# Fused top-k attention and GELU MLP: MLP pieces held behind the transposes, and x divided one or two rounds of DVE later, in the early slots

## The chip, the core and the metric

The kernel runs on one core of one Trainium2 chip. The core has five engines, each with a queue of its own that it works through in program order: PE (TensorE, matrix products; PEld is its loading of stationary operands), DVE (VectorE), ACT (ScalarE), POOL (GpSimd) and SP (SyncE, which here only issues DMAs). They wait for each other through semaphores. The metric is the device time of one execution in microseconds (us), smaller being better.

## The reference

Two stages, all in float32:

```python
scores = q @ k.T / sqrt(64)                       # 8 batches, 8 heads, 576 x 576
kth    = the 32nd largest score of each row
attn   = softmax(where(scores >= kth, scores, -1e9))
x      = (attn @ v) -> (4608 tokens, 512)          # heads side by side
g      = gelu_exact(x @ w_in)                      # w_in 512 x 2048
out    = g @ w_out                                 # w_out 2048 x 512
```

## The kernel before

**Items and slots.** The attention is cut into items: 128 rows of one pair of heads (576 rows make four items and a tail of 64 rows). A slot is one turn of the main loop and works on several items at different stages. In slot n of the first batch (`early_slot`, n = 0 to 17) the engines issue, in this order:

1. POOL adds the parts of one weight unit (`weights_add`, L235): the weights arrive as float32 words, are cut into two parts that PE multiplies well (ACT at L211, L214 and, in early units, L220; DVE at L216 in later units) and put together. A unit is two blocks of 128 x 512 of w_in or w_out; `made` is the set of units whose addition has been issued. 16 units are added in slots 1 to 16.
2. `larger(n+1)` on DVE (L420), `scores(n+2)`: PE multiplies q and k (the last keys at L347, the others at L384) and ACT copies the result (L355, L392).
3. `attend(n-2)`: PE multiplies the transposed exponentials with v into the tile o (L643), ACT copies o to xT (L661). The rows are not yet divided by their sum: a matmul with the inverse sums spreads these over o's other half (`dividing`, L656), and DVE multiplies (`copy_x`, L662). One MLP piece stands between o and the spread.
4. `top_k(n)`: DVE's search, a Python generator. A round is two `max` (L464: the eight largest of each head's row) and two `match_replace` (L467: take them out). There are six rounds for a paired item, the last ones without a replace; then DVE makes the inverse sums of item n-1 (`last`, L498) and the k-th value (L481, L482). The generator yields behind the first round; there the caller issues `copy_x` (so L662 stands behind one round in DVE's queue), and sets `ready`, the number of tokens whose x is complete.
5. `softmax(n-1)` for two heads on ACT (L511, L512), one part of the next weight unit (L211), two MLP pieces.
6. `transposes(n-1)`: PE transposes the exponentials in three pieces, two of four blocks (L573, one for each head) and the tail (L547), each followed by one MLP piece; ACT copies them to pt (L599, L557). The pieces of `transpose_qk` (L295, ACT's copies at L300) stand around them.
7. the other MLP pieces of the slot, the rest of the search, the weights' other parts, GELUs that have become due (`run_gelus`, ACT at L746, with an ACT table load ahead and one behind), `threshold` (POOL, L491, L492), from item 16 on `normalise` (POOL, L523), `sum_up` (POOL, L427), and the loads of the next slots.

**MLP pieces.** The MLP is a list `pieces` in a fixed order. A first-product piece (`l1_piece`, L726) is four matmuls of 128 x 128 in the first row tiles; a second-product piece (`full_piece`, L818) is one of 128 x 512. `mlp(n)` issues the next n pieces, as long as the slot's room (`left`) lasts, the piece's tokens are `ready`, and all its weight units are in `made`. With room left over, step 7 issues the rest. MLP work starts in slot 5 (`FIRST`). In slots 2 to 4 PE multiplies dummy tiles to stay busy.

**Rows of tokens.** In the first batch four consecutive items (the four pairs of heads) give a row tile of 128 tokens; in slots 5, 9, 13 and 17 `copy_x` completes such a row and `ready` goes up.

**Buffers.** Two score-sized PSUM tiles (`pr`, `l1`) and three banks; with MLP work only two banks (`z`, `y2`) go in turn to t_ps, o, tp_qk and tp_t, so the bank of o is free for the next but one user only when L662 has read it.

The slots in the trace of before, by the start of L420 on DVE, in us: slot 5 at 60.17, 6 at 69.24, 7 at 80.50, 8 at 90.16, 9 at 104.11, 10 at 117.96, 11 at 130.33, 12 at 140.40, 13 at 152.77, 14 at 164.97, 15 at 174.95, 16 at 186.18, 17 at 197.97, and the first slot of the later loop at 208.98. ACT's and PE's part of a slot starts about then. Behind the early slots a second loop works on the same stages in another order; there attention and MLP pieces share PE to the end.

Of the kernel before, what the change touches and what calls it, by code (L numbers as in the profile page):

```python
# [14 lines left out]
def kernel(  # L15
# [30 lines left out]
    NP = H // 2  # L46
# [106 lines left out]
    EARLY = NP * NM  # L153
# [14 lines left out]
    unit_in = UNIT_IN.get  # L168
# [30 lines left out]
    def parts(u):  # L199

        t, dst = words[u], weights_of(u)[3].bitcast(i32)
        return t[:, :, 0::2], t.bitcast(mybir.dt.int16)[:, :, 2::4], t[:, :, 1::2], dst

    def weights_size(u, part=None):


        if u not in words:
            return
        w, first, below, d = parts(u)
        if part != 1:  # L210
            nc.scalar.activation(below, first, func=AF.Prelu, bias=high, scale=2.0**-40, alpha=2.0**40)  # L211
        if part == 0:
            return
        nc.scalar.activation(d, below, func=AF.Prelu, bias=low, scale=2.0**59, alpha=2.0**-40)  # L214
        if on_dve(u):
            nc.vector.tensor_scalar(  # L216
                w.bitcast(i32), w.bitcast(u32), 2.0**-13, None, op0=ALU.mult
            )
        else:
            nc.scalar.activation(w.bitcast(i32), w.bitcast(u32), func=AF.Copy, scale=2.0**-13)  # L220

    def on_dve(u):

        return SLOT_OF[u] in ON_DVE

    def waits(u):

        return False

    made = set()  # L230

    def weights_add(u):
        if u in words:
            w, _, _, d = parts(u)
            nc.gpsimd.tensor_tensor(d, d, w.bitcast(i32), op=ALU.add)  # L235
        made.add(u)
# [172 lines left out]
    def paired(i):  # L409

        return PAIRED <= i < N and i not in SINGLE
# [5 lines left out]
    def larger(i):  # L417

        if paired(i):
            nc.vector.tensor_tensor(lists_of[i][:, 0], *halves_of(i), op=ALU.max)  # L420
# [16 lines left out]
    def top_k(i, last):  # L437


        stat_of[i] = st = {  # L440
            "first": work.tile([P, 2, 8], f32, tag="first", name="first"),
            "kth": work.tile([P, 2], f32, tag="kth", name="kth"),
            "neg": work.tile([P, 2], f32, tag="neg", name="neg"),
            "bias": work.tile([P, 2], f32, tag="bias", name="bias"),
            "den": work.tile([P, 2], f32, tag="den", name="den"),
            "rden": work.tile([P, 2], f32, tag="rden", name="rden"),
        }
        half_k = TOPK // 2
        top = work.tile([P, 2, TOPK - 8], f32, tag="top", bufs=1, name="top")
        low = work.tile([P, 2, half_k], f32, tag="low", bufs=1, name="low")  # L450
        into = [st["first"]] + [top[:, :, 8 * r : 8 * r + 8] for r in range(TOPK // 8 - 1)]
        if paired(i):
            t = lists_of.pop(i)
            rounds = [(t[:, 0], t[:, 0], x) for x in into]
            rounds += [(t[:, 1], t[:, 1], low[:, :, 8 * r : 8 * r + 8]) for r in range(half_k // 8)]
            ends = (len(into) - 1, len(rounds) - 1)
        else:
            s = S_of[i].rearrange("p (e n) -> p e n", e=2)
            t = work.tile([P, 2, S], f32, tag="lists", name="rest")
            rounds = [(s if r == 0 else t, t, x) for r, x in enumerate(into)]  # L460
            ends = (len(rounds) - 1,)
        for r, (src, dst, x) in enumerate(rounds):
            for e in range(2):
                nc.vector.max(x[:, e], src[:, e])  # L464
            if r not in ends:
                for e in range(2):
                    nc.vector.match_replace(dst[:, e], x[:, e], src[:, e], LOWEST)  # L467
            if r == len(rounds) - 1:
                last()
            if r == 0:  # L470
                yield

        if not paired(i):
            st["kth"] = top[:, :, TOPK - 9]
            return
        upper = top[:, :, half_k - 8 :]
        backwards = bass.AP(
            tensor=low.tensor, offset=low.offset + half_k - 1,
            ap=[list(low.ap[0]), [half_k, 2], [-1, half_k]],
        )  # L480
        nc.vector.tensor_tensor(upper, upper, backwards, op=ALU.max)  # L481
        nc.vector.tensor_reduce(  # L482
            st["kth"].rearrange("p (e x) -> p e x", x=1), upper, mybir.AxisListType.X, ALU.min
        )
# [9 lines left out]
    def inverse(i):  # L494
        if i < 0 or i >= N:
            return
        st = stat_of[i]
        nc.vector.reciprocal(st["rden"], st["den"])  # L498
# [7 lines left out]
    def softmax(i, e):  # L506

        if i < 0 or i >= N:
            return
        st, s = stat_of[i], row(i, e)  # L510
        nc.scalar.activation(s, s, func=AF.Prelu, bias=st["neg"][:, e : e + 1], scale=1.0, alpha=STEEP)  # L511
        nc.scalar.activation(  # L512
            s, s, func=AF.Exp, bias=st["bias"][:, e : e + 1], scale=1.0,
            accum_out=st["den"][:, e : e + 1],
        )
# [94 lines left out]
    def copy_x():  # L610
        while copies:
            copies.pop()()
# [83 lines left out]
    for base in range(0, NT, RING):  # L696
        whole = [(0, 256), (256, 256)] if base else [(t * P, P) for t in range(NM)]
# [317 lines left out]
    def run_gelus():  # L1015
        while waiting:
            u = waiting.pop(0)
            if u in HELD:
                gelus(u - 2)
            gelus(u)  # L1020
            if eager[0]:
                run_small(9)

    def run_ends():
        while ends:
            ends.pop(0)()

    def run_small(room):

        while summing:  # L1030
            sums(summing.pop(0))
            room -= 4
        while small and room > 0:
            n, f = small.pop(0)
            f()
            room -= n
# [10 lines left out]
    pieces = [x for y in blocks for x in y]  # L1047
    done = [0]

    def mlp(n):  # L1050
        for _ in range(n):
            if done[0] >= len(pieces) or pieces[done[0]][0] > ready[0] or left[0] <= 0:
                return
            if not all(w in made for w in pieces[done[0]][1]):
                return
            pieces[done[0]][2]()
            done[0] += 1
            left[0] -= 1
            if eager[0]:
                run_gelus()  # L1060
                run_small(9)


    ready, left = [0], [0]
    SPREAD = (12, 30)

    def room_in(n):

        x = n - START - 1
        if n < SPREAD[0]:  # L1070
            return min(7 if n < 9 else 6, sum(sizes[:4]) - done[0])
        if n < SPREAD[1]:
            ends = sum(sizes[:4]), sum(sizes[: SPREAD[1] - START - 1])
            part = (n - SPREAD[0] + 1) / (SPREAD[1] - SPREAD[0])
            return min(10, round(ends[0] + part * (ends[1] - ends[0])) - done[0])
        if x >= len(sizes):
            return 0
        return sizes[x] + (1 if x % 2 == 0 else -1)
# [62 lines left out]
    def early_slot(n):  # L1141

        left[0] = room_in(n) if n >= FIRST else 0
        begun[0] = n >= FIRST
        if not waits(unit_in(n)):
            weights_add(unit_in(n))
        larger(n + 1)
        scores(n + 2)
        product = attend(n - 2)
        mlp(1)  # L1150
        while dividing:
            dividing.pop()()
        searches = top_k(n, lambda: inverse(n - 1))
        next(searches)
        copy_x()
        ready[0] = n_tok[0]
        softmax(n - 1, 0)
        softmax(n - 1, 1)
        u = unit_in(n + 1)
        if u is not None:  # L1160
            weights_size(u, 0)
        mlp(2)
        if n < FIRST:
            keep_busy(6 if product else 12, ident)
        prep = prep_in.pop(n, [])
        for piece in prep[:1]:
            piece(None)
        tr = transposes(n - 1) if n - 1 < EARLY else []
        for piece in tr:
            piece()  # L1170
            mlp(1)
        for piece in prep[1:]:
            piece(None)
            mlp(1)
        if n < FIRST:
            keep_busy(8, ident)
        smaller(n + 1)
        add_small(n - 1)
        mlp(left[0])
        run_ends()  # L1180
        for _ in searches:
            pass
        if u is not None:
            weights_size(u, 1)
        run_gelus()
        threshold(n)
        normalise(n - 1)
        sum_up(n + 2)
        run_small(6)
        next_loads(n)  # L1190
# [5 lines left out]
    for n in range(LAST_EARLY + 1, ahead):  # L1196
# [16 lines left out]
        tr = transposes(n - 2)  # L1213
# [78 lines left out]
```

## Time and profile before

| what | value |
|---|---|
| time, median of 3 runs | 1569.61 us (1567.76 to 1569.66) |
| the profiled execution's own time | 1569.94 us |
| its span, first to last instruction | 1567.5 us |
| mean granted PE clock | 0.992 |
| span from 0 to 212 us | first batch, weights and the first MLP pieces |

The profile's rows read as follows. In order of time: start in us, duration in us, engine, line, operation, output<-input, shape, xcount of merged instructions, and in brackets the idle time of the engine before it with what ended it. Each float32 matmul is two records (x8 are four matmuls). In the waits view: who waited for whom, us in total, times, the longest. In the windows view: a stretch of the span and the busy time of each engine in it, then the clock granted to PE (1.00 is full), the DMA share and GB/s. The page's PEclk row cuts the span into 40 slices of 39.2 us; each digit is the granted clock in tenths.

### The profile page before, as it was taken

What the parts mean: (1) busy time and instruction counts of PE and PEld (TensorE: products, weight loads), DVE (VectorE), ACT (ScalarE), POOL (GpSimd) and SP (SyncE); (2) the same over time, 40 slices, a digit from 0 to 9 for tenths busy, and PEclk for the clock granted to TensorE, in tenths of its full rate; (3) what the DMA queues carried; (4) which work ended last, traced back from release to release, by engine and by line L of the source; (5) the groups of instructions that cost most, each with busy time, mean ns of one, the idle gap of its engine ahead of it and who ended that gap; (6) DMA issues with size and microseconds to landing.
All of it is one profiled execution on the core that took longest, in us unless ns stands there. A gap on an engine that the chain in (4) does not pass through costs nothing.

```text
span 1567.5 us, 28535 instructions
## 1 busy us (share of the span) xinstructions
PE 1521.3 (97%) x9478; PEld 1184.5 (76%) x9478; DVE 1335.6 (85%) x4605; ACT 1157.4 (74%) x2030; POOL 1096.1 (70%) x1253
## 2 busy tenths in 40 slices
PE   8979999999999999999999999999999999999998
PEld 6756667657777778887777778787777777787887
DVE  7978889899989997998989997988998998888700
ACT  6978867677777778777777778777777778777720
POOL 4646556556687877777787877786778786876732
PEclk9979999999999999999999999999999999999999
DMA  6432310011101111011200111001210111000000
GB/s 178 143 98 97 85 45 8 8 30 35 35 15 24 32 35 31 1 30 38 39 22 16 30 31 38 8 17 36 39 24 18 27 30 31 15 1 14 8 14 13
DMA packets 184243, 56.37 MB, mean 36 GB/s; under 512 B 175008, under 2 KB 175584, under 8 KB 184096
## 3 DMA queue, kind: packets, MB, share of 16 engines
q1 hardware_dynamic: 180720, 52.23, 14.1%
q10 hardware_dynamic: 3152, 2.00, 0.4%
q8 instruction: 74, 1.21, 0.3%
q14 instruction: 73, 0.60, 0.1%
q0 software_dynamic: 224, 0.33, 0.1%
HBM read 45.08 MB, written 9.44 MB: 35 GB/s over the span
## 4 chain that ended last, share of the span: by engine, by line
PE 71%; DVE 7%; POOL 6%; ACT 2%; issue 1%; SPq 0%; DMA 0%; DVEq 0%; POOLq 0%
PE h_ps L726 26%; PE y_ps L879 14%; PE o L643 7%; PE tp L573 6%; PE s_ps L384 5%; PE seven L877 2%; PE y_ps L818 2%; DVE top L464 2%; POOL s L523 2%; DVE rest L467 1%; PE tp_t L347 1%; PE y_ps L841 1%; PE y_ps L844 1%; PE o L672 1%; DVE lists L467 1%
## 5 line engine op out<-in xcount | busy, mean ns | idle before, releaser
L726 PE MATMUL h_ps<-xT,w_in_sb 128*128 128x256 f32 (+1 forms) x2688 | 530.6, 348 | 0.4 <-DVE xT L662 0.3
L726 PEld LDWEIGHTS h_ps<-xT,w_in_sb 128*128 128x128 f32 x2688 | 434.6, 191 | 65.3 <-issue 24.6
L464 DVE MAX8 top<-lists 128x8 f32<-128x288 f32 x798 | 323.8, 447 | 0.0
L523 POOL TENSOR_TENSOR s<-s,rden 128x1152 f32<-128x1152 f32 x128 | 269.1, 2102 | 0.3 <-DVE rden L498 0.3
L512 ACT ACTIVATE s<-s,bias 128x576 f32<-128x576 f32 x288 | 223.4, 776 | 12.0
L467 DVE MATCH_REPLACE8 lists<-top,lists 128x288 f32<-128x288 f32 x532 | 231.6, 443 | 0.0
L511 ACT ACTIVATE s<-s,neg 128x576 f32<-128x576 f32 x288 | 225.7, 784 | 4.2 <-POOL neg L491 4.0
L464 DVE MAX8 low<-lists 128x8 f32<-128x288 f32 x532 | 214.8, 446 | 0.0
L589 ACT COPY pt<-tp 128x1024 f32<-128x1024 f32 x128 | 130.0, 1016 | 101.8 <-PE tp L573 101.8
L504 POOL TENSOR_SCALAR den<-den 128x2 f32<-128x2 f32 x144 | 31.4, 218 | 237.6 <-ACT s L512 233.0
L435 POOL TENSOR_TENSOR lists<-lists 128x576 int32<-128x576 int32 x133 | 187.6, 1410 | 4.4
L427 POOL TENSOR_TENSOR lists<-s 128x576 int32<-128x576 int32 x133 | 187.0, 1406 | 0.0
L491 POOL TENSOR_SCALAR neg<-kth 128x2 f32<-128x2 f32 x133 | 85.2, 641 | 140.2 <-DVE kth L482 131.3
L573 PE MATMUL tp<-ident,s 128*128 128x128 f32 x1152 | 153.7, 274 | 5.5 <-ACT s L512 5.4
L643 PEld LDWEIGHTS o<-pt,raw_v 128*64 128x64 f32 x1440 | 93.1, 137 | 87.0 <-issue 46.8
L643 PE MATMUL o<-pt,raw_v 128*64 128x256 f32 (+1 forms) x1440 | 154.8, 362 | 0.0
L573 PEld LDWEIGHTS tp<-ident,s 128*128 128x128 f32 x1152 | 135.4, 142 | 23.9 <-ACT s L512 8.1
L392 ACT ACTIVATE s<-s_ps 128x1024 f32<-128x1024 f32 x127 | 124.9, 1026 | 21.9 <-PE s_ps L384 21.1
L384 PE MATMUL s_ps<-kt,qm 64*128 64x512 f32 x512 | 131.9, 625 | 4.5 <-ACT pt L589 2.9
L879 PE MATMUL y_ps<-w_out_sb,sum 128*128 128x256 f32 x448 | 133.2, 379 | 0.0
L498 DVE RECIPROCAL rden<-den 128x2 f32<-128x2 f32 x144 | 23.1, 160 | 118.2 <-POOL den L504 117.3
L467 DVE MATCH_REPLACE8 lists<-low,lists 128x288 f32<-128x288 f32 x266 | 115.9, 443 | 0.0
(168 smaller groups left out, 2756.3 us busy)
## 6 DMA issues: line engine op xcount, KB each, us to landing
raw_v<-in_v_dram SPq DMA_DIRECT2D x64, 128.0 KB, 2.4
w_out_sb<-in_moe_w_in_dram SPq DMA_DIRECT2D x14, 511.8 KB, 4.9
out_dram<-late SPq DMA_DIRECT2D x26, 256.0 KB, 2.1
raw_q<-in_q_dram SPq DMA_DIRECT2D x96, 64.0 KB, 2.1
raw_k<-in_k_dram SPq DMA_DIRECT2D x96, 64.0 KB, 2.1
w_out_sb<-in_moe_w_out_dram SPq DMA_DIRECT2D x10, 511.8 KB, 4.3
w_sum<-in_moe_w_out_dram SPq DMA_DIRECT2D x4, 511.8 KB, 5.5
raw_q<-in_q_dram SPq DMA_DIRECT2D x96, 8.0 KB, 1.9
```

Of the source, the lines that this page charges most:

```text
L384: nc.tensor.matmul(s_ps[:, e], lhsT=q_t[rows, :], rhs=kt[rows, 0:SM], start=True, stop=True)
L427: nc.gpsimd.tensor_tensor(t[:, 1].bitcast(i32), a.bitcast(i32), b.bitcast(i32), op=ALU.add)
L435: nc.gpsimd.tensor_tensor(both, both, top, op=ALU.subtract)
L464: nc.vector.max(x[:, e], src[:, e])
L467: nc.vector.match_replace(dst[:, e], x[:, e], src[:, e], LOWEST)
L511: nc.scalar.activation(s, s, func=AF.Prelu, bias=st["neg"][:, e : e + 1], scale=1.0, alpha=STEEP)
L512: nc.scalar.activation(s, s, func=AF.Exp, bias=st["bias"][:, e : e + 1], scale=1.0, accum_out=st["den"][:, e : e + 1],)
L523: nc.gpsimd.tensor_tensor(s, s, wide, op=ALU.mult)
L573: nc.tensor.transpose(tp[:, j * P : (j + 1) * P], s[:, first + j * P : first + (j + 1) * P], ident)
L643: nc.tensor.matmul(o[e * D : (e + 1) * D, 0:n], lhsT=vt[:, j, e, :], rhs=pt[:, e * NM + j if j < NM else 2 * NM, x], start=(j == 0), stop= ...
L726: nc.tensor.matmul(h_tile(u)[:, i, :], lhsT=w_in_sb[:, ko, f * P : (f + 1) * P], rhs=xT[:, ko, c0 : c0 + n], start=(ko == 0), stop=(ko == ...
L879: nc.tensor.matmul(acc[names][:, k], lhsT=lhsT, rhs=rhs, start=(j == 0 and k == 0), stop=(j == FT // 2 - 1 and k == 1),)
```

## The change

Two edits in `early_slot`, with a helper of each:

- At the start of a slot `known` becomes a copy of `made` as it was before this slot's weight unit is added. `mlp` takes a piece only if its units are in `known`; from the last transpose of the slot on (`known[0] = None`) it goes by `made` again. So pieces that need the unit added in the same slot come behind the transposes; pieces that don't need it stay where they were.
- `top_k` yields behind every round, and `early_slot` asks for three rounds ahead of `copy_x`, or for two where the slot completes a row of tokens (`whole`). The rounds themselves, their operands and their number stay.

`waits`, which always gave False, is removed. The lines behind it move up by four; lines are named as in the kernel before.

```diff
@@ top_k
-            if r == 0:
-                yield
+            yield
@@ mlp
-            if not all(w in made for w in pieces[done[0]][1]):
+            if not all(w in (known[0] or made) for w in pieces[done[0]][1]):
...
-    ready, left = [0], [0]
+    ready, left, known = [0], [0], [None]
@@ early_slot
-        if not waits(unit_in(n)):
-            weights_add(unit_in(n))
+        known[0] = set(made)
+        weights_add(unit_in(n))
...
         searches = top_k(n, lambda: inverse(n - 1))
-        next(searches)
+        whole = n - 2 < EARLY and (n - 1) % NP == 0
+        for _ in range(2 if whole else 3):
+            next(searches)
         copy_x()
...
         tr = transposes(n - 1) if n - 1 < EARLY else []
-        for piece in tr:
+        for x, piece in enumerate(tr):
             piece()
+            if x == len(tr) - 1:
+                known[0] = None
             mlp(1)
+        known[0] = None
```

More of the change, by code (lines that the diff above doesn't have):

```diff
@@ L224, in on_dve @@
         return SLOT_OF[u] in ON_DVE
-    def waits(u):
-        return False
     made = set()
```

## The prediction

> **What bounds the kernel now.** I read the page first, then the waits in the first batch (60 to 212 us), then that stretch in order of time, engine by engine.
>
> ```profile
> span 1567.5 us, 28535 instructions
> ...
> PE 1521.3 (97%) x9478; PEld 1184.5 (76%) x9478; DVE 1335.6 (85%) x4605; ACT 1157.4 (74%) x2030; POOL 1096.1 (70%) x1253
> ...
> PEclk9979999999999999999999999999999999999999
> ```
>
> PE is the bound. All its work is issued in program order, so whatever PE loses to waiting or to a low clock is paid at the end. It loses 1567.5 - 1521.3 = 46 us, and the granted clock is low in one slice only, the third (78 to 118 us). The edits touch the 18 early slots alone (to 209 us); behind them PE's order is unchanged and PE is the engine that the others follow. So I work out how much earlier PE arrives there.
>
> ```profile
> DVE xT L662 <- PE o L656: 24.6, 11, 4.2
> ```
>
> This is the wait that the second edit aims at: DVE stands 24.6 us in 11 stalls before the division of x. But a DVE stall costs time only where PE, or something that PE waits for, follows from it:
>
> ```profile
> 120.00:130.00 10.00, 10.00 (x93) 8.72 (x91) 7.34 (x28) 8.55 (x14) 4.17 (x5) 1.00 0.18 40
> ```
>
> The columns are PE, PEld, DVE, ACT, POOL busy, then the granted clock. PE is busy all of 10 us at full clock while DVE is busy 7.34: there DVE waits for PE, and ending its stall gives nothing. What can be gained lies in slots 6 to 9 (69 to 118 us), where PE idles and its clock falls:
>
> ```profile
> 80.60:84.00 3.40, 0.97 (x12) 0.49 (x9) 3.40 (x12) 3.32 (x8) 3.33 (x4) 1.00 0.12 22
> 84.00:101.00 17.00, 13.26 (x68) 10.15 (x67) 12.76 (x46) 10.33 (x17) 9.33 (x9) 0.60 0.37 124
> 104.50:107.90 3.40, 1.90 (x24) 1.07 (x20) 1.94 (x7) 3.37 (x5) 3.40 (x3) 1.00 0.00 0
> ...
> 111.30:114.70 3.40, 3.40 (x18) 3.40 (x18) 3.40 (x14) 3.35 (x7) 0.22 (x1) 0.50 0.47 189
> 142.00:145.40 3.40, 1.71 (x7) 0.74 (x8) 0.79 (x4) 3.39 (x8) 3.40 (x3) 1.00 0.00 0
> 145.40:148.80 3.40, 3.40 (x6) 1.25 (x6) 3.40 (x14) 3.30 (x5) 0.88 (x1) 0.51 0.81 279
> ```
>
> The clock falls behind 3.4 us in which PE was busy 0.97 us (at 84.0) and 1.71 us (at 145.4), not behind 1.90 us; it is back after a stretch that PE fills.
>
> **The change, part by part.** In the built programs PE's order differs in three slots only: in 6 and 8 four MLP pieces (16 matmuls) go behind the transposes, in 16 two pieces do. On DVE one instruction per slot moves back by one round (slots 5, 9, 13, 17) or two. ACT, POOL and SP keep their order, so no DMA issue passes another.
>
> Slot 5 (a whole row of tokens is ready, so its pieces read x at once):
>
> ```profile
> 62.75 1.38 PE L726 MATMUL h_ps<-xT,w_in_sb 128*128 128x128 f32 x10 [0.34 <-DVE xT L662]
> 62.61 0.81 DVE L464 MAX8 top<-lists 128x8 f32<-128x288 f32 x2
> ...
> 64.19 0.81 DVE L464 MAX8 top<-lists 128x8 f32<-128x288 f32 x2
> ```
>
> A round is 64.19 - 62.61 = 1.58 us. x now comes one round later, and PE, which already waits for it, **loses 1.58 us**. Nothing hides it, and DVE gains nothing, since it did not stall there.
>
> Slot 6:
>
> ```profile
> 73.17 0.78 ACT L512 ACTIVATE s<-s,bias 128x576 f32<-128x576 f32 x1
> ...
> 74.74 0.78 ACT L512 ACTIVATE s<-s,bias 128x576 f32<-128x576 f32 x1
> 73.49 2.10 PE L726 MATMUL y_ps<-xT,w_in_sb 128*128 128x128 f32 x16
> 75.43 0.60 PE L573 MATMUL tp<-ident,s 128*128 128x128 f32 x4
> 75.86 1.06 PE L726 MATMUL y_ps<-xT,w_in_sb 128*128 128x128 f32 x8
> ...
> 78.20 0.39 PE L347 MATMUL t_ps<-kt,qm 128*128 128x128 f32 x2
> ...
> 79.57 1.31 PE L643 MATMUL o<-pt,raw_v 128*64 128x128 f32 x20
> 82.83 0.77 ACT L512 ACTIVATE s<-s,bias 128x576 f32<-128x576 f32 x1
> 83.75 0.92 PE L573 MATMUL tp<-ident,s 128*128 128x128 f32 x4 [1.19 <-ACT s L512]
> ```
>
> ACT follows PE there and is 1.58 late too. Without a piece ahead of them the transposes wait for the two exponentials: the second starts at 74.74 + 1.58 = 76.3, its transposes 0.92 later (83.75 behind 82.83), at 77.25. Four transposes take 0.43 (75.43 to 75.86), the short ninth 0.1, and the 16 matmuls what is left of the 4.71 us from 73.49 to 78.20, some 3.65. Scores then start at 77.25 + 0.5 + 3.65 = 81.4, not 78.20: **3.2 late**. ACT stood behind PE there:
>
> ```profile
> 81.82 0.25 ACT L661 COPY xT<-o 128x128 f32<-128x128 f32 x1
> 91.51 0.27 ACT L661 COPY xT<-o 128x128 f32<-128x128 f32 x1 [0.82 <-PE o L643]
> 94.09 0.77 ACT L512 ACTIVATE s<-s,bias 128x576 f32<-128x576 f32 x1
> ...
> 94.87 1.21 ACT L211 ACTIVATE w_out_sb<-w_out_sb,high 128x1024 f32<-128x1024 int16 x1
> ```
>
> o starts 1.37 behind the scores (79.57 - 78.20) and takes 1.3: it ends at 84.05, and the copy starts there, not at 81.82. ACT and PE go through slot 7 hand in hand, so I carry **2.2 late** on: the copy of 91.51 comes at 93.7. DVE gets ahead, which nobody needs yet.
>
> Slot 8, where the gain is:
>
> ```profile
> 94.73 1.22 PE L726 MATMUL y_ps<-xT,w_in_sb 128*128 128x128 f32 x4 [2.63 <-POOL w_in_sb L235]
> ...
> 96.50 3.79 PE L726 MATMUL y_ps<-xT,w_in_sb 128*128 128x128 f32 x16
> ...
> 100.93 0.67 PE L573 MATMUL tp<-ident,s 128*128 128x128 f32 x4
> 101.17 0.58 ACT L300 COPY kt<-tp_qk 128x512 f32<-128x512 f32 x1 [5.09 <-PE tp_qk L295]
> 102.97 1.01 ACT L599 COPY pt<-tp 128x1024 f32<-128x1024 f32 x1 [1.21 <-PE tp L573]
> ...
> 107.58 1.09 ACT L746 ACTIVATE g<-y_ps 128x512 f32<-128x512 f32 x2
> ...
> 109.59 0.33 ACT L661 COPY xT<-o 128x128 f32<-128x128 f32 x1
> 109.97 0.44 PE L656 MATMUL o<-ident,rden 128*64 128x128 f32 x4 [3.57 <-ACT xT L661]
> ```
>
> Now PE waits 2.63 for the weights of that slot, multiplies at half clock (16 records in 3.79 us, in slot 6 in 2.10), and only at 100.93 transposes scores whose exponentials had started at 94.09 at the latest; from 102.97 ACT runs without a break to 109.59. Afterwards the spread follows o, and the second transposes come at 94.09 + 2.2 + 0.92 = 97.2. ACT's L211 (94.87 + 2.2, 1.2 long) ends at 98.2, the copy of keys takes 0.5, and the pt copy starts at 98.7: **4.3 early**. The four pieces run behind the tail transpose, from 98.0, at half clock (0.45 a matmul) until the clock returns. PE is full from 97.2, so it returns between about 100.6 and 104, by where in the 3.4 us steps PE stands; the pieces end at 103.1, 103.7 in the middle, or 104.6. The GELU of y_ps is due at 107.58 - 4.3 = 103.3 and waits for at most 1.3; scores and o (1.37 + 1.3) follow the pieces, so the copy of 109.59 comes at 105.8, 106.4 or 107.3: 3.8, 3.2 or 2.3 early. PE's wait of 3.57 is nearly gone, since o ends just before. So no empty stretch precedes slot 9, and the half clock of 111.3 to 114.7 falls away: it cost up to 1.7, but the transposes of that slot follow ACT's exponentials, so between 0 and 1.7 comes back; I take 0.9. The second round of slot 9 costs nothing: DVE reaches the division before the copy and still waits. At slot 10 PE is **4.7, 4.1 or 3.2 early**; I take 4.1. From there PE is full and DVE ahead, and the loads of w_out stand in SP's queue behind loads that follow PE's transposes, so they come as much earlier.
>
> Slot 16 and the end:
>
> ```profile
> 193.48 0.66 PE L573 MATMUL tp<-ident,s 128*128 128x128 f32 x4 [0.32 <-ACT s L512]
> 193.97 1.02 PE L818 MATMUL y_ps<-w_out_sb,g 128*128 128x512 f32 x2
> 195.05 0.66 PE L573 MATMUL tp<-ident,s 128*128 128x128 f32 x4
> ...
> 212.08 0.41 PE L550 MATMUL tp_t<-ident,s 128*64 128x128 f32 x2 [0.53 <-POOL s L523]
> ```
>
> The piece between the transposes filled their wait for the second exponential. It goes behind, the 1.08 us from 193.97 to 195.05 stay empty, and PE **loses 0.9** (ACT is at work without a break there, so nothing hides it). At 212.08 PE waited 0.53 for a POOL product that hangs on DVE's k-th value; DVE needs one round less behind its last division, so **0.5** returns. Sum: 1.58 and the rest of slots 5 to 9 make -4.1, then + 0.9 - 0.5 = **-3.7** (-4.3 to -2.8). The profiled execution took 1569.94 us, 2.4 more than its span; that gives 1566.2, and from the median of 1569.61, 1565.9.
>
> The Trainium skill bears on the clock ("TensorE: Matmul & The Clock Gate", Part 1: The HAM clock gate): a free-running window of about 3.4 us, half clock after an idle window, full clock after a busy one. The trace agrees with the window (3.4 us at half from 111.3, 17.0 = 5 x 3.4 from 84.0), but its clock fell without an idle one.
>
> **The rivals.** A: *the clock stays full*, if only a wholly empty step lowers it: no wait left in slots 7 and 8 is longer than 1.3 us.
>
> ```profile
> 87.53 2.08 PE L384 MATMUL s_ps<-kt,qm 64*128 64x512 f32 x4 [0.46 <-ACT pt L599]
> ```
>
> From these scores to the copy of 91.51 it is 3.98 at half clock, and would be some 2.4 (1.1 and 1.3): 1.6 less. The pieces end before the GELU is due, so the pt copy and all behind it come 5.9 early, and slot 10, with up to 1.1 of slot 9's clock, 7.0: -6.6, 1563.0. The page's rule gives this; the 0.97 and 1.71 above speak against it.
>
> B, the other side: *the clock falls already in slot 6.* Its emptiest 3.4 us (73.8 to 77.2) will hold some 1.6 us of PE work: 0.8 of a piece's four matmuls, 0.4 of spread (109.97), 0.4 of transposes. Below 1.71 the clock has fallen, at 1.90 not. If it falls there and returns only in slot 9: 16 matmuls at half (+3.6), scores and o of slot 7 (+1.7), all of slot 8's pieces at half (+1.4), slot 9 no better than now (+0.9): -3.7 + 7.6 = +3.9, 1573.5. Against it: the clock returns once PE fills 3.4 us, which these 16 matmuls do.
>
> C: *the delays of slots 5 and 6 eat the gain*: the late end (-2.8) and one 3.4 us step of half clock in slot 6 (+1.7): -1.1, 1568.5.
>
> D: *all DVE stalls are given back*: 1569.6 - 24.6 = 1545; against it stands the full PE of 120 to 130 us. That an edit does nothing is excluded: both move instructions in the built program.
>
> **How the numbers follow.** Forecast 0.56, A 0.08, B 0.10, C 0.24, D 0.02. About 0.2% (3.1 us) is what a measurement of this kernel can tell. Faster by more: forecast without its late end (0.52), A and D: 0.62. Within: C and that end, 0.28. Slower: B, 0.10. The range leaves out B and D: from A, 1563.0, to 1569.0, just above C.
>
> **What would show it.** PE's wait for x in slot 5 near 1.9 us; scores of slot 7 at 81.4; the pt copy of slot 8 near 98.7; no wait for POOL weights in slot 8; no half clock in slot 9; L662's stalls moved to slots 9, 12, 13, 17, not gone. Wrong would be: half clock before 84 (B), none at all (A), or a PE in slots 10 to 15 that isn't full.

## The result, and the profile after

The changed kernel takes 1561.15 us (median of 4 runs, 1559.38 to 1562.20); the kernel before took 1568.89 (4 runs, 1567.76 to 1569.66) beside it. The ratio is 0.995, interval 0.9933 to 0.9967: 5.2 to 10.5 us less. The forecast had the sign, and about half of the size: 3.7 less, range to 1563.0. A second comparison, on another chip, gave 0.9965 (0.9952 to 0.9979), 3.3 to 7.5 us less. The profiled executions of two runs below, `known8` and `after_again`, took 3162 and 2614 us; they and their traces are left out of every number that follows.

The page of the changed kernel, to be held against the first rows of the prediction:

```profile
span 1559.1 us, 28536 instructions
...
PE 1514.1 (97%) x9478; PEld 1178.0 (76%) x9478; DVE 1336.6 (86%) x4605; ACT 1157.0 (74%) x2030; POOL 1095.8 (70%) x1253
...
PEclk9999999999999999999999999999999999999999
```

PE is busy 7.2 us less (1521.3 - 1514.1) for the same instructions. So most of the gain shows up as work done at a higher clock; the third slice has lost its 7. What raised the clock is a question for the experiments. The lines of the changed kernel stand 4 or 5 lower: L657 is the division that was L662, L721 the MLP piece that was L726.

Where along the early slots does the time come from? PE's scores (t_ps) and ACT's pt copy serve as landmarks. The table gives the start of each in us, the forecast as the prediction worked it out (the time before plus its shift), and one experiment, `early_one`, which is told below.

| landmark | before | forecast | after | early_one |
|---|---|---|---|---|
| scores, slot 6 | 69.42 | 71.0 | 68.64 | 71.93 |
| scores, slot 7 | 78.20 | 81.4 | 79.06 | 82.35 |
| pt copy, slot 8 | 102.97 | 98.7 | 96.14 | 99.64 |
| scores, slot 10 | 118.65 | 114.6 | 110.89 | 114.37 |
| scores, slot 13 | 153.31 | | 146.44 | 148.66 |
| scores, slot 17 | 197.91 | | 191.87 | 194.07 |

The changed kernel left the forecast already in slot 5, and by slot 10 it was 3.7 us ahead of it. DVE's timeline has the reason, in a slot that the prediction never looked at. Before, slot 2, and the first instruction of slot 5:

```profile
35.23 0.29 DVE L662 TENSOR_TENSOR xT<-xT,o 128x128 f32<-128x128 f32 x1 [2.31 <-PE o L656]
...
60.17 0.75 DVE L420 TENSOR_TENSOR lists<-s 128x576 f32<-128x576 f32 x1
```

After, the same two and the division of slot 5:

```profile
35.77 0.28 DVE L657 TENSOR_TENSOR xT<-xT,o 128x128 f32<-128x128 f32 x1
...
57.54 0.75 DVE L416 TENSOR_TENSOR lists<-s 128x576 f32<-128x576 f32 x1
...
61.49 0.29 DVE L657 TENSOR_TENSOR xT<-xT,o 128x128 f32<-128x128 f32 x1
```

In slot 2 DVE had stood 2.31 us for o. With two rounds more ahead of the division that stall is gone, DVE enters slot 5 2.63 us earlier (60.17 - 57.54), and there the second round (1.58) is more than paid for: x is divided at 61.49, before it was at 62.42. PE's wait for x, which was to grow from 0.34 to 1.9, vanishes instead.

Slot 8 on PE after the change:

```profile
93.12 0.66 PE L568 MATMUL tp<-ident,s 128*128 128x128 f32 x4 [0.60 <-ACT s L507]
94.68 0.66 PE L568 MATMUL tp<-ident,s 128*128 128x128 f32 x4 [0.91 <-ACT s L507]
95.18 0.27 PE L542 MATMUL tp_t<-ident,s 128*128 128x128 f32 x1
95.29 3.74 PE L721 MATMUL y_ps<-xT,w_in_sb 128*128 128x128 f32 x32
98.86 0.39 PE L343 MATMUL t_ps<-kt,qm 128*128 128x128 f32 x2
```

The transposes follow the exponentials, the 32 records of the pieces come behind them without a wait for POOL, and at full clock (0.117 us each, where the forecast had them at half). The clock itself, in its own steps of 3.41 us (busy PE second, the granted clock third from the end). Before:

```profile
84.00:87.41 3.41, 2.43 (x11) 1.73 (x9) 3.41 (x13) 3.32 (x6) 2.80 (x3) 0.50 0.32 77
87.41:90.82 3.41, 3.29 (x16) 1.79 (x18) 3.38 (x12) 2.54 (x5) 1.09 (x2) 0.50 0.59 235
90.82:94.23 3.41, 1.28 (x16) 0.91 (x12) 1.67 (x7) 2.61 (x6) 3.41 (x3) 1.00 0.00 0
94.23:97.64 3.41, 2.91 (x13) 2.36 (x14) 0.95 (x4) 1.85 (x3) 2.03 (x3) 0.50 0.58 166
97.64:101.05 3.41, 3.41 (x18) 3.41 (x18) 3.41 (x14) 0.00 (x0) 0.00 (x0) 0.50 0.35 142
```

After:

```profile
83.59:87.00 3.41, 1.65 (x11) 1.22 (x11) 3.38 (x14) 3.38 (x7) 0.71 (x2) 0.99 0.59 228
87.00:90.41 3.41, 3.08 (x14) 1.57 (x16) 3.41 (x14) 2.69 (x5) 3.41 (x4) 0.51 0.00 0
90.41:93.82 3.41, 2.40 (x26) 1.51 (x22) 3.41 (x14) 2.60 (x7) 2.43 (x2) 1.00 0.33 100
```

The prediction read 84 to 101 us as one stretch at half clock. It was two stretches of two steps, with a full one between (90.82 to 94.23), and the second fell out of PE's wait for POOL in slot 8. After the change there is a single step at half in this stretch.

Behind slot 10 three things move the sum. In slot 16 the gap between the transposes appears as forecast (t_ps loses 0.83 from slot 16 to slot 17). The wait of 0.53 at 212.08 is gone, as forecast. And slot 12 brings one that was not seen. ACT's timeline after:

```profile
129.40 1.21 ACT L211 ACTIVATE w_out_sb<-w_out_sb,high 128x1024 f32<-128x1024 int16 x1 [2.25 <-DMA w_out_sb<-in_moe_w_out_dram]
130.51 0.57 ACT L296 COPY kt<-tp_qk 128x512 f32<-128x512 f32 x1
130.97 1.02 ACT L594 COPY pt<-tp 128x1024 f32<-128x1024 f32 x1
```

and PE's, behind ACT's copy of keys:

```profile
131.13 0.49 PE L343 MATMUL t_ps<-kt,qm 128*128 128x128 f32 x2 [1.74 <-ACT kt L296]
```

Before, ACT's wait for that load was 1.30, and PE's 0.81. PE arrives 7.76 us earlier at slot 10, but by slot 13 its lead is 6.87: 0.89 goes here.

The spans differ by 8.4 us (1567.5 and 1559.1), of which 6.8 are there at the pt copy at 207.53 (214.29 before). The last 1.6 is luck of the clock. In both kernels PE waits 2.4 us near the end; the clock falls behind that wait in some executions and not in others. Before, behind that wait:

```profile
1555.20:1558.60 3.40, 3.33 (x8) 2.71 (x9) 0.00 (x0) 0.37 (x1) 2.09 (x4) 0.51 0.00 0
```

After:

```profile
1549.10:1552.50 3.40, 3.40 (x18) 2.99 (x17) 0.00 (x0) 0.74 (x2) 1.43 (x3) 1.00 0.00 0
```

From that pt copy to the end it is 1351.5 to 1351.8 us or 1353.2 to 1353.4 us in all twelve traces, with nothing between, and both values occur in kernels with either edit. So of the 4.7 us by which the span lies below the forecast (1567.5 - 3.7 = 1563.8, measured 1559.1), 3.1 are there at the pt copy of 207.53 (forecast 210.6), and 1.6 are this luck.

Of the waits that the second edit aims at, less than half is left under that name, and 4.9 us more in two stalls that the same row books to ACT (60 to 212 us):

```profile
DVE xT L657 <- PE o L651: 11.5, 7, 3.4
...
DVE xT L657 <- ACT s L506: 4.9, 2, 3.0
```

So 8.2 us of DVE's stalls from 60 us on are gone. The experiments tell which mattered.

### The profile page after: what moved, and what is told of

It is laid out like the page before. It is cut to its first block, busy times and chain, and to the rows that moved or that the text cites. A ratio compares the mean times of both kernels' runs of the same rounds, so it can differ in the third digit from the quotient of the medians.

```text
span 1559.1 us, 28536 instructions
## 1 busy us (share of the span) xinstructions
PE 1514.1 (97%) x9478; PEld 1178.0 (76%) x9478; DVE 1336.6 (86%) x4605; ACT 1157.0 (74%) x2030; POOL 1095.8 (70%) x1253
## 4 chain that ended last, share of the span: by engine, by line
PE 72%; DVE 7%; POOL 6%; ACT 2%; issue 1%; DVEq 0%; POOLq 0%
PE h_ps L721 26%; PE y_ps L874 15%; PE o L638 7%; PE tp L568 6%; PE s_ps L380 6%; PE y_ps L813 3%; PE seven L872 2%; DVE top L460 2%; POOL s L518 2%; DVE rest L463 2%; PE tp_t L343 1%; PE y_ps L836 1%; PE y_ps L839 1%; PE o L667 1%; PE tp_t L542 1%
## 5 line engine op out<-in xcount | busy, mean ns | idle before, releaser
L721 PE MATMUL h_ps<-xT,w_in_sb 128*128 128x256 f32 (+1 forms) x2688 | 529.3, 347 | 0.0
L721 PEld LDWEIGHTS h_ps<-xT,w_in_sb 128*128 128x128 f32 x2688 | 433.5, 191 | 64.6 <-issue 24.6
```

The lines of the kernel that those rows point to most:

```text
L721: nc.tensor.matmul(h_tile(u)[:, i, :], lhsT=w_in_sb[:, ko, f * P : (f + 1) * P], rhs=xT[:, ko, c0 : c0 + n], start=(ko == 0), stop=(ko == ...
```

## The experiments

The theory after the result, called Lead: the gain is (1) slot 8's transposes, no longer behind pieces that wait for weights, and (2) DVE's lead out of slot 2, which pays for slot 5's second round. Rivals: Stalls (DVE's later stalls are what counts), Clock (the half clock alone), Order (the held pieces alone). Ratios are to the kernel before on the same chip, with their intervals; its medians were 1567.6, 1567.8 and 1566.8 us in the three groups of four. The profiled execution of before took 1569.94 us, as long as the longest of its 20 runs in the first group (1564.33 to 1569.99). So a landmark's lead over it can be some 2 us more than a typical one: known_only is 6.5 ahead of it at the end of the batch and gains 4.4. In the traces of these kernels, lines are numbered as in the kernel before (with the filling, those behind L602 are five higher).

### Each edit alone: known_only and dve_only

Both are edits of the changed kernel.

```diff
-        for _ in range(2 if whole else 3):
+        for _ in range(1):
             next(searches)
```

> The changed kernel with the division of x back behind DVE's first round; only the MLP pieces are held back. Theory Lead (the gain is slot 8's transposes, which no longer stand behind pieces that wait for weights, plus 2.3 to 2.6 us by which DVE enters slot 5 earlier because its stall of slot 2 is gone): the stall of 2.31 us in slot 2 is back, PE waits about 0.3 us for x in slot 5 as before, the pt copy of slot 8 still comes 4 us or more earlier than 102.97, and the half clock of slots 8 and 9 is short; 1562 to 1564 us, 0 to 2.5 behind the changed kernel. Theory Stalls (the gain is DVE's stalls in slots 6 to 17): no gain, 1568 to 1570. Theory Order (the held pieces alone carry the gain): 1561, as the changed kernel.

Measured: 1563.01, ratio 0.9972 (0.9961 to 0.9982). The stall of slot 2 is back (2.31 at 35.08), the pt copy of slot 8 comes at 97.37, 5.6 earlier than before, scores of slot 10 at 112.11. This is what Lead expected, and Stalls misses. Order (1561, as the changed kernel) is not ruled out by this run: the interval overlaps that of the changed kernel's second comparison (0.9952 to 0.9979). The next two runs speak against it.

```diff
-        known[0] = set(made)
+        known[0] = None
```

> The changed kernel with the pieces where they were; only the division of x moves to the second or third round. Theory Lead: in slot 8 PE still waits 2 to 3 us for POOL's weights ahead of the transposes, the clock is at half for some 17 us behind 84, and DVE's lead buys at most 0.5 in slot 5 and 0.5 at slot 18: 1567.5 to 1569, within 0.2% of before. Theory Stalls: most of the gain is here, 1561 to 1563. Theory Order: 1568 to 1570.

Measured: 1563.66, ratio 0.9972 (0.9961 to 0.9983). This was a miss for Lead, and for Order; Stalls (1561 to 1563) came nearest. The second edit alone gains as much as the first alone, while both together gain less than the sum of the two. By the pt copy that ends the first batch (214.29 before) the changed kernel, at 207.53, is even level with known_only (207.78) and dve_only (207.47); the 1.2 and 1.5 us by which it leads them at slot 10 are lost by then, to the longer wait for the load, to a half step in slot 12 that known_only's execution did not have, and, against dve_only, to the held pieces of slot 16. PE no longer waits for POOL in slot 8, although the pieces stand where they stood. POOL before, ahead of the weights of slot 8 (L235):

```profile
89.73 0.59 POOL L491 TENSOR_SCALAR neg<-kth 128x2 f32<-128x2 f32 x1 [2.84 <-DVE kth L482]
90.28 0.68 POOL L492 TENSOR_TENSOR bias<-kth,first 128x2 f32<-128x2 f32 x1
90.92 1.40 POOL L427 TENSOR_TENSOR lists<-s 128x576 int32<-128x576 int32 x1
92.29 2.39 POOL L235 TENSOR_TENSOR w_in_sb<-w_in_sb,w_out_sb 128x1024 int32<-128x1024 int32 x1
```

POOL with the second edit alone:

```profile
85.56 0.59 POOL L491 TENSOR_SCALAR neg<-kth 128x2 f32<-128x2 f32 x1 [1.02 <-DVE kth L482]
...
88.12 2.39 POOL L235 TENSOR_TENSOR w_in_sb<-w_in_sb,w_out_sb 128x1024 int32<-128x1024 int32 x1
```

and PE's first two pieces of slot 8, with no wait ahead of or between them (before, 2.63 between them):

```profile
90.86 1.28 PE L726 MATMUL y_ps<-xT,w_in_sb 128*128 128x128 f32 x8
```

POOL works in order, and ahead of the weights stands an instruction that waits for DVE's k-th value. DVE reaches slot 8 at 86.00 and not at 90.16, so the weights are added 4.2 us earlier and PE finds them ready. The two edits remove the same wait of 2.63, the one by not asking for the weights, the other by having them in time. The prediction had said of DVE in slot 6 that it "gets ahead, which nobody needs yet"; POOL needs it.

### The failed step by itself: early_one

```diff
-        for _ in range(2 if whole else 3):
+        for _ in range(1 if n < 5 else 2 if whole else 3):
             next(searches)
```

> The changed kernel with slots 2 to 4 back at one round; slot 5 and all later ones keep two or three. This puts DVE into slot 5 as late as the prediction assumed. Theory Lead: the stall of 2.31 us in slot 2 is back, L420 of slot 5 starts near 60.2 and not 57.5, PE waits 1.6 to 1.9 us for x in slot 5, scores of slot 7 start near 81.4 as predicted; 1562.5 to 1565, some 1.5 to 3 behind the changed kernel. Theories Stalls and Order: slots 2 to 4 hold no stall that matters, 1561, as the changed kernel.

Measured: 1564.64, ratio 0.9983 (0.9974 to 0.9992): 2.7 us less than before, where the changed kernel's two ratios make 5.5 and 7.8. Stalls and Order, which expected no difference from the changed kernel, both miss. This kernel has the whole change except in slots 2 to 4, so DVE comes into slot 5 as the prediction assumed. And the prediction then holds: PE's wait for x was to be "near 1.9 us", and is

```profile
63.83 1.22 PE L726 MATMUL h_ps<-xT,w_in_sb 128*128 128x128 f32 x4 [1.93 <-DVE xT L662]
```

The last two columns of the table above differ by this edit alone: 3.3 us at slots 6 and 7, 3.5 at slots 8 and 10, and 2.2 behind slot 12. There the changed kernel waits longer for a load (0.4 of PE's time, below); the other 0.9 goes in slot 12 itself, where a half step of the clock falls at another place in the two executions. Against its forecast the kernel is 0.9 late in slots 6 to 8 (the step from 63.52 to 66.93 ran at 0.51, behind one with 1.30 us of work: a half clock in slot 5 that the forecast lacked) and level at slot 10, 4.28 early where 4.1 was forecast. That it is level is luck in part: the late 0.9 is made good by the pieces of slot 8, which run faster than forecast (below).

### Which slots of the second edit count: dve_2to4 and dve_5on

Both are edits of the kernel before.

```diff
-        next(searches)
+        for _ in range(3 if n < 5 else 1):
+            next(searches)
```

> The kernel before with one edit: in slots 2 to 4 x is divided behind DVE's third round; from slot 5 on behind the first, and no piece is held back. Theory Lead, amended by the second-edit-alone run (1563.7): DVE's 2.3 to 2.6 us out of slot 2 reach POOL through the k-th values, POOL adds the weights of slot 8 that much earlier, and PE's wait of 2.63 for them goes. So nearly the whole gain of the second edit is in these three slots: 1563 to 1565, L420 of slot 5 near 57.5, no wait for POOL in slot 8. Theory Stalls (the division's later place in slots 6 to 17 counts): 1567 to 1569, as before.

Measured: 1567.15, ratio 0.9995 (0.9985 to 1.0005), no gain that can be told. A miss for Lead. The lead is won (the division of slot 5 is at 61.27), and given back at once, since DVE now stalls there itself. DVE, slots 5 and 6:

```profile
61.27 0.29 DVE L662 TENSOR_TENSOR xT<-xT,o 128x128 f32<-128x128 f32 x1 [1.60 <-PE o L656]
...
72.68 0.29 DVE L662 TENSOR_TENSOR xT<-xT,o 128x128 f32<-128x128 f32 x1 [2.26 <-PE o L656]
```

DVE is in slot 8 at 89.15, only 1.0 ahead of before, and PE again waits 2.30 for POOL's weights.

```diff
-        next(searches)
+        for _ in range(1 if n < 5 else 2 if whole else 3):
+            next(searches)
```

> The kernel before with one edit: from slot 5 on x is divided behind the second or third round; in slots 2 to 4 behind the first, and no piece is held back. Theory Lead: the stall of 2.31 us in slot 2 stays, PE waits some 1.9 us for x in slot 5, DVE comes into slot 8 no earlier than before, so POOL's weights still hold PE by 1.5 to 3 us; 1567 to 1570, no gain or a loss. Theory Stalls: 1563 to 1565, the gain of the second edit.

Measured: 1566.05, ratio 0.9990 (0.9981 to 0.9998). A second miss for Lead, though a small one. As it expected, PE waits 1.92 for x in slot 5 (slot 6's scores come at 72.30, 2.9 late), and DVE comes into slot 8 no earlier (89.89). The wait for POOL, though, is gone, for PE has become late enough. Scores of slot 10 stand at 116.27, with dve_2to4 at 116.15, with both halves at 112.40 (before 118.65). The two halves give 2.4, 2.5 and together 6.25: a lead has to be won in slot 2 and kept through slots 5 and 6, and only then does it reach POOL and PE in slot 8. So Stalls was right in part, for slots 2 to 6; the stalls behind them (slots 9, 12, 13, 16 and 17 still hold 1.9 to 3.4 us each after the change) were not tested by themselves.

### The clock by itself: before_fill

An edit of the kernel before.

```diff
-            return [lambda: turn_over(pr[0][:, 0], 0), lambda: turn_over(pr[0][:, 1], 1), ends]
+            def fill(e, m):
+                for _ in range(m if i == 6 else 0):
+                    nc.tensor.matmul(pr[0][:, e, 0:P], lhsT=ident, rhs=ident, start=True, stop=True)
+                turn_over(pr[0][:, e], e)
+
+            return [lambda: fill(0, 8), lambda: fill(1, 6), ends]
```

> The kernel before with 14 additional matmuls of 128x128 whose result is overwritten, in slot 7 alone, where PE waits for the exponentials (8 ahead of the first transposes, 6 ahead of the second), so that PE is busy for some 1 us more in the stretch of 3.4 us after which the clock fell. It prices the clock by itself. If the clock is what both edits gain by (theory Clock): no half clock from 84 to 101, and 1562 to 1564, the gain of either edit. Theory Lead: the wait of 2.63 us for POOL's weights stays, since DVE and POOL do not move; with full clock the 16 matmuls behind it take 2.1 and not 3.8, slot 9 starts 2 to 3 us earlier: 1564.5 to 1566. If the clock falls all the same: 1567 to 1568.

Measured: 1567.10, ratio 0.9997 (0.9987 to 1.0006). The filling did hold the clock, in the kernel before:

```profile
85.98:89.39 3.41, 2.64 (x25) 1.69 (x25) 3.38 (x15) 3.06 (x6) 0.66 (x2) 1.00 0.79 307
89.39:92.80 3.41, 1.33 (x18) 0.96 (x13) 2.92 (x9) 3.22 (x7) 3.26 (x4) 1.00 0.00 0
92.80:96.21 3.41, 1.66 (x8) 1.23 (x8) 0.00 (x0) 1.89 (x3) 3.28 (x3) 0.51 0.19 34
```

and PE, done sooner, then stood 3.84 and not 2.63 us for POOL's weights, behind which the clock fell after all:

```profile
94.56 1.22 PE L731 MATMUL y_ps<-xT,w_in_sb 128*128 128x128 f32 x4 [3.84 <-POOL w_in_sb L235]
```

Clock alone falls as a theory: as long as the weights hold PE, a faster clock ahead of them buys a longer wait.

### The held pieces in slot 8 alone: known8 and known8_again

```diff
-        known[0] = set(made)
+        known[0] = set(made) if n == 8 else None
```

> The changed kernel with the pieces held back in slot 8 alone; in slots 6 and 16 they stand between the transposes as before. Theory Lead: slot 16 gets its 0.8 to 0.9 us back, and slot 6 some 0.5 to 1.6 (there the changed kernel's scores of slot 7 lost 1.6 against its own slot 6), of which ACT's chain to slot 8 passes on about half; 1559 to 1560.5. Theory Order (the held pieces of slot 6 are needed as well): 1561 or later. Theory Clock (the gain is the half clock that ends at 90.4 and not at 101): 1561 if the clock still returns by 92, 1565 or more if it does not.

Measured: 1558.87, ratio 0.9953 (0.9939 to 0.9967).

> The changed kernel with the pieces held back in slot 8 alone, once more: beside the changed kernel on the same chip, and for its profile. Theory Lead: 0.9 us come back in slot 16 (no wait of 0.91 between its transposes), and slot 6 is as with the second edit alone (scores of slot 7 near 77.2, not 79.06); 0.9 to 1.7 less than the changed kernel. Theory Order: the same as the changed kernel.

Measured: 1559.17, ratio 0.9951 (0.9939 to 0.9964), 2.5 below the changed kernel on the same chip (`after_again`, below). Scores of slot 7 come at 77.30 (79.06 after), and from slot 16's scores to slot 17's it is 11.98 us and not 12.86. So what the prediction charged to slots 6 and 16 was real, and the change pays it for nothing: only slot 8's pieces have weights to wait for. Order misses here too, and so does Clock: this trace has three steps at half from 84 to 98 us where the changed kernel has one, and still reaches the last pt copy of the batch 2.35 earlier (205.18 and 207.53).

### The load of slot 12: after_load, and known8_load

The changed kernel issues this load at the end of slot 10 (123.25 us), this edit at the start of the slot (114.81).

```diff
         weights_add(unit_in(n))
+        if n == 10:
+            load_weights(12)
...
-            if m > 2 and m == n + 2:
+            if m > 2 and m == n + 2 != 12:
```

> The changed kernel with one thing altered: the load of the weights that ACT scales in slot 11 is issued at the start of slot 10. Theory Lead: the changed kernel arrives at that load 7.8 us earlier and the load only 6.8 earlier, since it stands in SP's queue behind loads that wait for PE; ACT's wait of 2.25 us and PE's of 1.74 us go, 1.7 to 2.2 us less than the changed kernel. If ACT's wait only hides another (DVE's k-th value, POOL's weights): no change.

Measured: 1559.64, ratio 0.9955 (0.9942 to 0.9967), 2.0 below the changed kernel on the same chip. ACT runs on without the wait:

```profile
127.64 0.19 ACT L512 ACTIVATION_READ_ACCUMULATOR s<-s,bias 128x1 f32 x1
127.74 1.26 ACT L211 ACTIVATE w_out_sb<-w_out_sb,high 128x1024 f32<-128x1024 int16 x1
128.87 0.58 ACT L300 COPY kt<-tp_qk 128x512 f32<-128x512 f32 x1
130.00 1.01 ACT L599 COPY pt<-tp 128x1024 f32<-128x1024 f32 x1 [0.56 <-PE tp L573]
```

From slot 10's scores to slot 13's it is 33.24 us (111.58 to 144.82) and not 35.55. The prediction had said that these loads "come as much earlier" as PE; they stand in SP's queue behind loads that PE's transposes release. This one was issued 7.5 earlier (130.72 before), took 0.7 longer to land, and so came 6.8 earlier where ACT came 7.8 earlier.

> The changed kernel with the pieces held back in slot 8 alone, and the load of the weights that ACT scales in slot 11 issued at the start of slot 10, ahead of loads on SP's queue that wait for PE. Theory Lead: ACT's wait of 2.25 us for that load (at 129.40) goes; ACT works without a break from there to the pt copy of slot 13, so 1.7 to 2.2 us come back against the run with slot 8 alone (1559.8): 1557.5 to 1558.5. If the wait was hidden behind DVE or POOL: 1559.5 to 1560.

Measured (slot 8 alone, and this load): 1558.06, ratio 0.9938 (0.9924 to 0.9951). The time is the expected one, but it does not show that the load brought 1.7 to 2.2 us: the interval overlaps that of slot 8 alone. In known8_again ACT's wait was 1.25 and not 2.25 us; without it PE does slots 10 to 12 in 18.34 and not 19.30 us, but this execution then has a half step in slots 12 and 13 that known8_again has not, and ends the batch at 204.83 (205.18).

### All of it, with the clock held: known8_load_fill

The same filling as above, with 4 and 3 matmuls, in known8_load.

> The version with the pieces held back in slot 8 alone and the early load (1558.1), with 7 additional matmuls of 128x128, overwritten, in the two waits of slot 7 for the exponentials (1.19 and 0.91 us). In the kernel before such matmuls only made PE's wait for POOL's weights longer (2.63 to 3.84); here nothing waits for POOL in slot 8. Theory Lead plus clock: the half clock of 85 to 92 goes and the scores and o of slot 7 take 2.4 and not 4.3 us: 0.8 to 1.5 us less, 1556.5 to 1557.3. If ACT or DVE paces slots 7 and 8 all the same: 1558.

Measured: 1555.77 (1555.33 to 1557.57), ratio 0.9930 (0.9917 to 0.9944): the fastest of the kernels here, 5.9 below the changed kernel on the same chip. PE in slot 7:

```profile
81.89 1.16 PE L607 MATMUL tp<-ident 128*128 128x128 f32 x8
83.14 0.66 PE L573 MATMUL tp<-ident,s 128*128 128x128 f32 x4
83.64 0.83 PE L607 MATMUL tp<-ident 128*128 128x128 f32 x6
84.72 0.65 PE L573 MATMUL tp<-ident,s 128*128 128x128 f32 x4 [0.25 <-ACT s L512]
```

and the clock over the first batch, for this kernel

```profile
60.00:150.00 90.00, 79.36 (x646) 60.47 (x643) 81.76 (x292) 82.51 (x133) 55.81 (x52) 1.00 0.35 110
```

and for known8_load

```profile
60.00:150.00 90.00, 78.45 (x615) 58.84 (x610) 79.00 (x281) 79.99 (x130) 55.30 (x50) 0.94 0.34 108
```

The filling lies in waits that were there anyhow, no step falls to half from 60 to 150 us, and scores of slot 10 come at 108.91 and not 110.66. Against known8_load, which ran on another chip, the ratios make it 1.3 us, within the 0.8 to 1.5 expected; by the pt copy that ends the first batch (204.83 and 202.21) it is 2.6, since the half step of slots 12 and 13 went too. The intervals of the two ratios overlap; what sets the kernels apart is the mean granted clock, 0.999 in four of the five runs here and 0.995 to 0.996 in all six of known8_load. What bought nothing in the kernel before pays here, where nothing waits for POOL.

### after_again

The changed kernel once more.

> The changed kernel itself, once more, beside the three below on one chip. Theory Lead: 0.4 to 0.5% below before, as in the first comparison. Its tail shows whether the half-clock step at the very end (1.7 us, in the profiled execution of before and not in that of the changed kernel) belongs to the kernel or to the single execution: from the pt copy of slot 18 to the end 1351.6 us without it, 1353.3 with it; if it belongs to the execution, either can come, and the landmarks up to 212 us stay within 0.5 us of the first profile unless a half-clock step falls elsewhere.

Measured: 1561.65, ratio 0.9965 (0.9952 to 0.9979). Whether its tail took the half step stays open.

## Why the prediction was wrong, point by point

The step that failed is that of slot 5: "x now comes one round later, and PE, which already waits for it, **loses 1.58 us**. Nothing hides it, and DVE gains nothing, since it did not stall there." DVE did not stall *there*, but in slot 2, 2.31 us, and the edit changes slot 2 as well. The prediction said of the edit that it moves "one instruction per slot", and read the list of stalls from 60 us on, behind the place where the first of them stood. early_one puts that stall back: 3.5 us at slot 10, and the time returns to within 1.0 us of the forecast shift (2.7 where 3.7 was forecast). Of the 4.7 us by which the span lies below the forecast, this stall makes 2.2 (last pt copy at 209.73 and 207.53), and the tail's luck 1.6; the other 0.9 is spread over the slots behind slot 9 (209.73 where the forecast gives 210.6).

- *Slot 6* (scores of slot 7 3.2 late): with the premise restored 4.15 late; in the changed kernel 0.86 late, since PE came 0.78 early into slot 6. The piece's own cost, 1.64, was right (forecast 3.2 - 1.58 = 1.6).
- *Slot 8* (pt copy 4.3 early): 6.8 early; 3.3 with the premise restored. The order of events was right. The size of the clock was not: the pieces ran at full clock, because the half clock behind 94 us was itself a result of the wait that the change removes. The prediction had read a mean clock of 0.60 from 84 to 101 us as one long stretch at half; one of its five steps ran at 1.00.
- *Slot 9* (0.9 of half clock saved; the second round costs nothing): no half clock there; right, with some luck: PE still waited 1.60 us for ACT (at 103.15), and the step before held 1.8 us of work, among the values behind which the clock went either way (last section).
- *"DVE gets ahead, which nobody needs yet"*: wrong. POOL needs it for the weights of slot 8 (dve_only). In the changed kernel the pieces don't ask for them, so here it costs the forecast nothing.
- *Slot 16* (loses 0.9): 0.83 to 0.88; right. *212 us* (0.5 returns): 0.69 from slot 17's scores to it; right.
- *Loads "come as much earlier"*: wrong in slot 12, 0.9 lost, 2.3 to be had (slots 10 to 13 in after_load).
- *L662's stalls moved, not gone*: right for slots 9, 12, 13 and 17, and slot 16 has one more of 2.97; their sum fell from 24.6 to 16.4.

The rivals. A, the clock stays full, gave 1563.0, nearest to the result, but not by its mechanism: the clock fell in slot 7 (to 0.51 at 87.00). B did not come: the clock's own step there, 73.36 to 76.77, held 2.50 us of PE work where B had put 1.6. Of C, early_one has the half step, in slot 5 and not in 6, but not the size: 2.7 less, where C had 1.1. D did not come: 16.4 us of the stalls are still there, and the time is 16 us above D's 1545.

## What to carry to other kernels

When an edit sits in a loop, list what it meets in every iteration, from the first one on: a stall that is taken out early is a lead that pays for a cost later, and a lead counts until the next stall of the same engine. Before calling an engine's lead useless, follow each queue behind it in order (here DVE's k-th value, POOL's next instruction, the weights, PE). Two edits that remove one wait by different means don't add up.

## What the runs showed of the hardware

The granted clock went in steps of 3.413 us that run on through the kernel (before, the falls at 84.0 and 1555.1 us lie 431 of them apart), and PE's busy time in one step went with what came next. The figures are good to about 0.1 us, for the edges of the steps are placed to within some 0.06. In the eleven traces with falls from 60 to 150 us (31 falls), the clock fell behind steps with 0.00 to 1.9 us of PE work; every full-clock step with 1.5 or less was followed by a fall, none with 2.0 or more, and those between went either way. A step at half was followed by full clock where PE was busy 3.0 us or more (1.00 behind 3.08 and 3.29 above; 3.04 in known8_load), and by another half one at 2.95 or less (2.43 and 2.91 above, 2.95 in dve_only). The Trainium skill ("TensorE: Matmul & The Clock Gate", Part 1: The HAM clock gate) has the fall behind an idle window and the return behind a busy one; the traces agree on the length and on its running free, but here half a step of work was too little to keep the clock, and nine tenths enough to win it back. That fits known8_load_fill, in which seven matmuls in two waits kept all of the first batch at full clock. Why a step with 1.88 fell (91.41 in after_load) and one with 1.64 did not (132.14 in known8_again) stays open.
